# Routed experts in order of kept tokens, with a 224-wide and a 96-wide second item

## The chip, the cores and the metric

The kernel runs on one core of a Trainium2 chip. The metric is device time of one execution in microseconds (us). Three timed executions of the kernel before gave 530.63, 530.70 and 531.04 us, median 530.7 us. A profile is one more execution, with its own time.

## The reference

Three layers in a row, in float32: attention with rotary positions over 2 batches of 576 tokens (8 heads of 64), a dense feed-forward layer 512 to 2048 to 512, and a layer of 8 routed experts, each 512 to 1024 to 512. The last is what this case is about:

```
    logits = x @ w_gate                      # 1152 tokens, 8 experts
    expert_idx = np.argmax(logits, axis=1)
    ...
    for i in range(N):
        e = expert_idx[i]
        if counts[e] < capacity:             # capacity = 288
            disp[e, counts[e]] = x[i]
            ...
    h = np.maximum(np.einsum('ecd,edf->ecf', disp, w1), 0.0)
    y = np.einsum('ecf,efd->ecd', h, w2)
    out[i] = gate_w[i] * y[expert_idx[i], pos[i]]   # kept tokens; the rest stay 0
```

The reference with its inputs sends the first 576 tokens to two experts (212 tokens to expert 3, 364 to expert 5, of which 288 are kept) and the second 576 to two others (509 to expert 0, of which 288 are kept, 67 to expert 4). So 855 rows of the output are written, and 297 stay zero.

## The kernel before

*Stages.* Attention; then the dense layer in three chunks of 480, 384 and 288 tokens (blocks of 96 tokens, CUTS), 16 slices of its hidden width each; then up to four routed *items* in straight code, and a loop (line 1048) for items that did not fit into them. An item is one expert with up to 288 slots (HALF). Of the 576 tokens of a batch the routing fills two items: items 0 and 1 after block 6 (in chunk 3's time), items 2 and 3 after chunk 3. With these inputs the items hold 212, 288, 288 and 67 tokens, in the order of the experts' numbers, and the loop runs zero times. Each item computes all 288 columns, whatever it holds.

*One item* (`second`, with `ffn`). Eight slices. A slice is one weight load of 512 KB (`wf`, line 965, issued by SP), cut into a high and a low float32r half (`hl`: line 671 on ACT, 672 on DVE), 12 matmuls into `h` (line 696; the high and low products over 4 blocks of 128), `gh` on ACT (721) and `gl` on DVE (722), and 12 matmuls into the four accumulators `y` (line 706). After the last slice `yt` copies (983), 12 transposes `tr` (991), three scalings by the gate (`row`, 997 and 999) and three indirect scatters to `out` (1000) on POOL. A slice's load is issued no earlier than the cut of the slice six before it (LEAD).

*Routing* (`route`, lines 776 to 920). A chain of some 74 short DVE operations, with matmuls for the ranks in between, from the logits to `r_at`, the slot of each token; then six indirect writes to the table `slots` in DRAM from POOL (871). On one partition DVE also makes `etab` (the expert of each item, 892) and `n`, the number of items (920).

*Gather.* SP loads an item's part of the table (`ent`, line 927: 288 slots of 16 bytes), POOL gathers three blocks of 96 rows (`got`, line 932), PE transposes them (`tg`, 949, four for each block) and ACT and DVE split them into `xt` (955, 956). Those transposes stand two slices before the end of the item ahead (`hook`).

*Order.* A scheduler writes each engine's order at build time, by a model of durations; instructions of one engine start in that order. SP's order holds the weight loads, the block stores `x<-row` (761), the `ent` loads and the loads of expert numbers (1013), POOL's the indirect DMAs. So a waiting `ent` load on SP holds the weight loads behind it.

Of the kernel before, what the change touches and what calls it, by code (L numbers as in the profile page):

```python
# [24 lines left out]
P = 128  # L25
# [8 lines left out]
ITEMS = 4 + 14  # L34
# [70 lines left out]
def consts():  # L105
# [16 lines left out]
    for b in range(B):  # L122
# [11 lines left out]
        (e[None, :] < e[:, None]).reshape(-1),  # L134
        np.repeat(np.arange(16)[:, None], E, 1).reshape(-1),
        np.repeat(e[None, :], 16, 0).reshape(-1),
        np.arange(16),
# [455 lines left out]
class Experts:  # L593


    def __init__(self, ctx, tc, d, cst, xt, weights):
# [19 lines left out]
        self.small = one.tile([TT, 48 + 64 + 128 + 128 + 16], F32, name="small")  # L616
# [5 lines left out]
        self.etab = one.tile([1, 20], I32, name="etab")  # L622
        self.loc = one.tile([1, B, 16], F32, name="loc")
        self.small_parts = {}
        at = 0
        for n, shape in (("rev", (NT, E)), ("low", (E, E)), ("k", (16, E)), ("e", (16, E)), ("i", (16,))):
# [47 lines left out]

    def ffn(self, x, slices, act, hook=None):
# [6 lines left out]
        for f in range(n + LAG):  # L682
# [4 lines left out]
            if f < n:  # L687
                hl = hls[f]
                h = self.ps_h.tile([P, 512], F32, tag="h", name="h")[:, 0:w]
                ops = [  # L690
                    (hl[:, i, j * P:(j + 1) * P], x[:, k, j, :])
                    for j in range(ND)
                    for i, k in ((0, 0), (0, 1), (1, 0))
                ]
                for m, (u, v) in enumerate(ops):
                    nc.tensor.matmul(h, u, v, start=m == 0, stop=m == len(ops) - 1)  # L696
                gh = self.g.tile([P, WIDE], F32R, name="gh")[:, 0:w]
                gl = self.g.tile([P, WIDE], F32R, name="gl")[:, 0:w]
                act(h, gh, gl, f)
                gs.append((gh, gl))  # L700
# [25 lines left out]
    def first(self, k0, k1, hook=None):  # L726
# [17 lines left out]
        for k in range(k0, k1):  # L744
            b, i = divmod(k, NT)
            cs = slice((k - k0) * TT, (k - k0 + 1) * TT)
            row = self.three.tile([TT, DM], F32, name="row")
# [15 lines left out]
    def route(self, b, L):  # L763
# [20 lines left out]

        big, col = lambda n: new(n, NT, E), lambda n: new(n, NT)
        big16 = lambda n: new(n, NT, E, dt=BF16)
        mx = col("mx")
        red(mx, L, ALU.max)
        ls, ex, sm, gate = big("ls"), big("ex"), col("sm"), col("gate")
        tt(ls, L, per(mx), ALU.subtract)  # L790
        nc.scalar.activation(out=ex, in_=ls, func=AF.Exp)
        red(sm, ex)
        ts(sm, sm, 1e-9, ALU.add)
        v.reciprocal(out=gate, in_=sm)
        sc, fm, oh = big("sc"), col("fm"), big("oh")
# [12 lines left out]
        found = oh16.rearrange("p (a k) e -> p a k e", a=2)  # L808
# [12 lines left out]
        cnt, left, tmp, tmp2 = new("cnt", E), new("left", E), big("tmp"), big("tmp2")  # L821
        v.tensor_copy(out=cnt, in_=pc[0:TT, 0:E])
        ts(left, self.carry, -1.0, ALU.mult, self.cap, ALU.add)
        tt(self.carry, self.carry, cnt, ALU.add)
        tt(tmp, rank, oh, ALU.mult)
        lr, keep = col("lr"), col("keep")
        red(lr, tmp)
        tt(tmp2, rank, every(left), ALU.is_lt)
        tt(tmp2, tmp2, oh, ALU.mult)
        red(keep, tmp2)  # L830
        kc, items, base = new("kc", E), new("items", E), new("base", E)
        ts(kc, left, 0.0, ALU.max)
        tt(kc, kc, cnt, ALU.min)
        ts(items, kc, 0.0, ALU.is_gt)
        more = new("more", E)
        ts(more, kc, float(HALF), ALU.is_gt)
        tt(items, items, more, ALU.add)
        sq = new("sq", E, E)
        tt(sq, sp["low"], items.unsqueeze(1).to_broadcast([TT, E, E]), ALU.mult)
        red(base, sq)  # L840
        ends, ni = new("ends", E), new("ni", 1)
        tt(ends, base, items, ALU.add)
        red(ni, items)
        jb, over = col("jb"), col("over")
        tt(tmp, oh, every(base), ALU.mult)
        red(jb, tmp)
        ts(over, lr, float(HALF), ALU.is_ge)
        tt(jb, jb, over, ALU.add)
        slot, few = col("slot"), col("few")
        ts(few, jb, 2.0, ALU.is_lt)  # L850
        off = new("off", 1)
        ts(off, self.xoff, -1.0, ALU.mult, 2.0 * b - 2.0, ALU.add)
        ts(few, few, off, ALU.mult)
        ts(few, few, self.xoff, ALU.add, 2.0, ALU.add)
        tt(slot, jb, few, ALU.add)
        tt(slot, slot, over, ALU.subtract)
        v.scalar_tensor_tensor(out=slot, in0=over, scalar=1.0, in1=slot, op0=ALU.mult, op1=ALU.add)
        ts(slot, slot, float(HALF), ALU.mult)
        tt(slot, slot, lr, ALU.add)
        ts(over, over, float(HALF), ALU.mult)  # L860
        tt(slot, slot, over, ALU.subtract)
        ts(keep, keep, -float(FAR), ALU.mult, float(FAR), ALU.add)
        tt(slot, slot, keep, ALU.add)
        at = new("at", NT, dt=I32)
        placed = v.tensor_copy(out=at, in_=slot)
# [16 lines left out]
        with self.tc.issue_after(placed.ins):  # L882

            k, e = sp["k"][0:1], sp["e"][0:1]
            m1, m2 = new("m1", 16, E, part=1), new("m2", 16, E, part=1)
            lo, hi = (x[0:1].unsqueeze(1).to_broadcast([1, 16, E]) for x in (base, ends))
            tt(m1, k, lo, ALU.is_ge)
            tt(m2, k, hi, ALU.is_lt)
            tt(m1, m1, m2, ALU.mult)
            tt(m1, m1, e, ALU.mult)  # L890
            red(self.loc[:, b], m1)
            v.tensor_copy(out=self.etab[:, 2 * b:2 * b + 2], in_=self.loc[:, b, 0:2])
            if b == 0:
                ts(self.xoff, ni, -2.0, ALU.add, 0.0, ALU.max)
                return

            x0 = self.xoff[0:1]
            z1 = new("z1", 16, part=1)
            lo2, hi2 = new("lo2", E, part=1), new("hi2", E, part=1)
            tt(lo2, base[0:1], x0.to_broadcast([1, E]), ALU.add)  # L900
            tt(hi2, ends[0:1], x0.to_broadcast([1, E]), ALU.add)
            lo, hi = (x.unsqueeze(1).to_broadcast([1, 16, E]) for x in (lo2, hi2))
            tt(m1, k, lo, ALU.is_ge)
            tt(m2, k, hi, ALU.is_lt)
            tt(m1, m1, m2, ALU.mult)
            tt(m1, m1, e, ALU.mult)
            red(z1, m1)
            late, lim = new("late", 16, part=1), new("lim", 1, part=1)
            ts(lim, x0, 2.0, ALU.add)
            ts(late, sp["i"][0:1], lim, ALU.is_ge)  # L910
# [3 lines left out]
            tt(z1, z1, late, ALU.add)  # L914
            v.tensor_copy(out=self.etab[:, 4:18], in_=z1[:, 2:16])
            n1 = new("n1", 1, part=1)
            ts(n1, ni[0:1], -2.0, ALU.add, 0.0, ALU.max)
            tt(n1, n1, x0, ALU.add)
            ts(n1, n1, 4.0, ALU.add)
            v.tensor_copy(out=self.etab[:, 18:19], in_=n1)  # L920
# [103 lines left out]
    def run(self):  # L1024
# [4 lines left out]
        def turn(i):  # L1029
            x[i] = self.turn(found[i][1], i)  # L1030
# [51 lines left out]
```

## Time and profile before

| | |
|---|---|
| timed, median of 3 | 530.7 us (530.63 to 531.04) |
| the profiled execution's own time | 531.68 us |
| its span in the trace | 530.0 us |
| PE busy | 489.3 us, 92% |
| DVE, ACT, POOL busy | 374.1, 275.7, 112.9 us |
| HBM, mean over the span | 97 GB/s |
| mean granted clock of TensorE | 0.983 of 2.4 GHz |

The span ends when the last instruction of the trace does; 1.68 us of the execution's own time lie around it. PE is the busiest engine in every stage but the last, so a place where PE stands still, or runs at half its clock, shows as time, and so does each matmul that goes. The matmuls overlap: the duration of one says less than the distance from start to start of a run of the same shape. In a row of the timeline `[2.28 <-DMA got<-x,ent]` means that the engine was idle 2.28 us before it, and what ended that.

### The profile page before, as it was taken

To read this page: it belongs to the slowest core of one execution; us is meant where nothing else is said; L and a number is where in the kernel's file an instruction comes from. 1 tells how busy PE (TensorE), PEld (TensorE's weight loads), DVE (VectorE), ACT (ScalarE), POOL (GpSimd) and SP (SyncE) were. 2 spreads that over 40 slices of the span, in tenths; PEclk is the share of its full clock that TensorE was granted. 3 is DMA by queue.
4 is the path that set the end of the run, shared out by engine and by line. 5 is a ranking of instruction groups with operands and counts; after the bars stand their busy time and mean duration, and the time that the engine had idled before them with its cause. 6 is when DMAs were issued, how large, how long until landed. Compare 5 with 4: busy or idle time off the path is not lost.

```text
span 530.0 us, 8969 instructions
## 1 busy us (share of the span) xinstructions
PE 489.3 (92%) x3306; PEld 440.8 (83%) x3306; DVE 374.1 (71%) x761; ACT 275.7 (52%) x520; POOL 112.9 (21%) x119
## 2 busy tenths in 40 slices
PE   1889999999999999999999999999899996999991
PEld 0768778778777788788899999999899985999991
DVE  6798898898789999998355343677456873565631
ACT  3567678667557534345543444655464532645421
POOL 5964534322211200000000000002510073120202
PEclk9999999999999999999999999999989997999996
DMA  7042332222043475661011400010495427564200
GB/s 246 0 110 77 101 94 67 79 51 71 4 130 121 151 278 179 238 238 41 0 31 53 171 1 1 16 46 2 142 288 151 153 58 228 177 190 153 86 1 14
DMA packets 21535, 56.16 MB, mean 106 GB/s; under 512 B 4996, under 2 KB 6180, under 8 KB 21488
## 3 DMA queue, kind: packets, MB, share of 16 engines
q1 hardware_dynamic: 19136, 50.91, 30.4%
q0 software_dynamic: 1920, 4.13, 2.8%
q8 instruction: 28, 0.46, 0.4%
q10 hardware_dynamic: 432, 0.51, 0.3%
q14 instruction: 19, 0.16, 0.1%
HBM read 44.38 MB, written 7.18 MB: 97 GB/s over the span
## 4 chain that ended last, share of the span: by engine, by line
PE 41%; issue 25%; DVE 17%; DMA 8%; ACT 4%; POOL 4%; POOLq 0%; SPq 0%; ACTq 0%; DVEq 0%
PE h L696 13%; PE y L706 12%; PE s L392 6%; PE pv L492 4%; DVE nm L396 3%; PE tp L441 3%; DMA raw<-in_w_in 2%; DMA qx<-qs 2%; DVE hl L297 2%; POOL out L1000 2%; PE tr L752 2%; DMA got<-x,ent 1%; POOL slots L871 1%; ACT pp L403 1%; DMA raw<-in_w_out 1%
## 5 line engine op out<-in xcount | busy, mean ns | idle before, releaser
L696 PE MATMUL h<-xt,hl 128*128 128x288 f32 (+2 forms) x960 | 181.1, 326 | 2.4 <-issue 1.8
L696 PEld LDWEIGHTS h<-xt,hl 128*128 128x128 f32 x960 | 152.2, 190 | 10.8 <-issue 3.3
L706 PE MATMUL y<-gh,hl 128*128 128x288 f32 (+2 forms) x640 | 142.0, 325 | 2.4 <-issue 2.0
L672 DVE TENSOR_TENSOR hl<-wf,hl 128x1024 fp32r<-128x1024 f32 x80 | 97.7, 1224 | 62.4 <-ACT hl L671 61.0
L671 ACT ACTIVATE hl<-wf 128x1024 fp32r<-128x1024 f32 x80 | 84.5, 1059 | 60.6 <-PE y L706 34.6
L706 PEld LDWEIGHTS y<-gh,hl 128*128 128x128 f32 x640 | 108.4, 191 | 5.9 <-issue 1.7
L706 PE MATMUL y<-gl,hl 128*128 128x288 f32 (+2 forms) x320 | 89.7, 324 | 1.1 <-issue 1.1
L396 DVE TENSOR_REDUCE nm<-s 128x1 f32<-128x576 f32 x72 | 53.8, 752 | 12.0 <-PE s L392 10.7
L706 PEld LDWEIGHTS y<-gl,hl 128*128 128x128 f32 x320 | 58.7, 191 | 3.5 <-issue 1.7
L403 ACT ACTIVATE pp<-s,nm 128x576 f32<-128x576 f32 x64 | 47.7, 745 | 23.9 <-DVE nm L396 23.4
L871 POOL DMA_INDIRECT slots<-entry,r_at x12 | 13.5, 1124 | 218.6 <-DVE r_m L776 180.8
L715 ACT ACTIVATE g<-h 128x480 f32<-128x480 f32 (+2 forms) x48 | 23.4, 490 | 61.0 <-PE h L696 50.2
L392 PE MATMUL s<-ks,qs 128*128 128x288 f32 (+1 forms) x168 | 53.0, 333 | 2.0 <-ACT pp L403 1.6
L392 PE MATMUL s<-ks,qx 128*128 128x288 f32 (+1 forms) x168 | 46.9, 306 | 3.2 <-DMA qx<-qs 2.4
L211 ACT ACTIVATE pt<-tp 128x512 f32<-128x512 f32 x56 | 33.1, 599 | 19.6 <-PE tp L441 19.0
L717 DVE TENSOR_TENSOR gl<-g,gh 128x480 fp32r<-128x480 f32 (+2 forms) x48 | 26.5, 554 | 22.2 <-ACT gh L716 22.0
L441 PE MATMUL tp<-ident,pp 128*128 128x128 f32 x256 | 39.8, 281 | 0.5 <-DVE ptr L213 0.5
L492 PE MATMUL pv<-pt,vr 128*64 128x288 f32 x256 | 39.1, 414 | 0.6 <-DVE pt L213 0.3
L392 PEld LDWEIGHTS s<-ks,qs 128*128 128x128 f32 x168 | 32.6, 195 | 8.2 <-ACT pp L403 3.6
L721 ACT ACTIVATE gh<-h 128x288 fp32r<-128x288 f32 x32 | 13.2, 412 | 45.8 <-PE h L696 31.9
L392 PEld LDWEIGHTS s<-ks,qx 128*128 128x128 f32 x168 | 32.8, 196 | 4.6 <-DMA qx<-qs 2.0
L441 PEld LDWEIGHTS tp<-ident,pp 128*128 128x128 f32 x256 | 30.5, 143 | 5.3 <-issue 2.6
(178 smaller groups left out, 593.3 us busy)
## 6 DMA issues: line engine op xcount, KB each, us to landing
wf<-in_w SPq DMA_DIRECT2D x32, 512.0 KB, 4.1
raw<-in_w_in SPq DMA_DIRECT2D x16, 512.0 KB, 3.9
raw<-in_w_out SPq DMA_DIRECT2D x16, 512.0 KB, 3.3
qx<-qs SPq DMA_DIRECT2D x14, 320.0 KB, 4.2
qk<-in_qk SPq DMA_DIRECT2D x12, 288.0 KB, 3.1
vr<-in_v SPq DMA_DIRECT2D x8, 320.0 KB
x<-row SPq DMA_DIRECT2D x12, 192.0 KB, 2.1
out<-zero SPq DMA_DIRECT2D x9, 256.0 KB, 2.9
```

Of the source, the lines that this page charges most:

```text
L211: return e.activation(out=out, in_=x, func=AF.Copy, **({} if scale is None else {"scale": scale}))
L392: nc.tensor.matmul(ps[:, n, c:c + w], x, ks[:, src:src + w], start=j == 0, stop=j == len(mine) - 1)
L396: nc.vector.tensor_reduce(out=nm, in_=ps[:, :, 0:HALF], axis=AX.XY, op=ALU.max, negate=True)
L403: nc.scalar.activation(out=out.rearrange("p (n k) -> p n k", n=2), in_=ps[:, :, 0:HALF], func=AF.Exp, bias=d["nm"][:, i:i + 1], accum_out= ...
L441: nc.tensor.transpose(t[:, kt], pp[:, h, h * 64 + kt * P:h * 64 + (kt + 1) * P], self.ident)
L492: nc.tensor.matmul(o[h * 64:h * 64 + 64], x, y, start=j < 2, stop=j > 7)
L671: nc.scalar.activation(out=hl[:, 0], in_=t, func=AF.Copy)
L672: self.last = nc.vector.tensor_tensor(out=hl[:, 1], in0=t, in1=hl[:, 0].bitcast(F32), op=ALU.subtract).ins
L696: nc.tensor.matmul(h, u, v, start=m == 0, stop=m == len(ops) - 1)
L706: nc.tensor.matmul(y[j][:, 0:w], u, v, start=f == LAG and m == 0, stop=f == n + LAG - 1 and m == 2)
L715: nc.scalar.activation(out=g, in_=h, func=AF.Gelu_apprx_sigmoid)
L717: nc.vector.tensor_tensor(out=gl, in0=g, in1=gh.bitcast(F32), op=ALU.subtract)
```

## The change

Seven parts.

1. Items of a batch are ordered by kept tokens (most first; `key`, `sq`), not by the number of the expert.
2. STATIC gives each of the four items its blocks: items 0 and 2 three of 96 tokens, item 1 two of 112 (224 columns), item 3 one of 96. Tokens of a second item beyond 224 or 96 go to an item of the loop (`more`, `extra`, `s1`, `s2`).
3. Item 3 is computed token-major (`few`): `y` is 96 tokens x 512, with `gh` and `gl` as the stationary operand and 512 columns of the weights moving, 3 matmuls a slice instead of 12; no `yt`, no `tr`; the scaling is halved between ACT and DVE; one scatter.
4. The routing chain is shorter: 57 operations up to `r_at` instead of 74. The gate's exponent, sum and reciprocal come after `r_at`.
5. `ent` loads are issued by POOL, not SP.
6. The number of an item's expert is loaded by SP without waiting for `ent` to have been issued.
7. The transposes `tg` may stand up to the end of the item ahead (hook 0 instead of 2).

```diff
+STATIC = (3, 96), (2, 112), (3, 96), (1, 96)
...
-        tt(sq, sp["low"], items.unsqueeze(1).to_broadcast([TT, E, E]), ALU.mult)
+        stt(key, kc, float(E), ALU.mult, sp["e"][:, 0, :], ALU.subtract)
+        wide = [TT, E, E]
+        tt(sq, key.unsqueeze(1).to_broadcast(wide), key.unsqueeze(2).to_broadcast(wide), ALU.is_gt)
+        tt(sq, sq, items.unsqueeze(1).to_broadcast(wide), ALU.mult)
         red(base, sq)
...
+        ts(back, ni, -float(HALF), ALU.mult, float(HALF + narrow), ALU.add)
+        ts(over, self.xoff, float(HALF), ALU.mult, float((2 - 2 * b) * HALF), ALU.add)
+        tt(over, over, back, ALU.subtract)
+        ts(s1, lin, float(first + HALF + narrow), ALU.is_ge, over, ALU.mult)
+        ts(s2, lin, float(first + 2 * HALF), ALU.is_ge, back, ALU.mult)
+        tt(lin, lin, s1, ALU.add)
+        tt(lin, lin, s2, ALU.add)
...
-        ent = self.three.tile([TT, 3, 4], I32, name="ent", bufs=5)
-        src = self.slots[bass.ds(item * HALF, HALF), :].rearrange("(i p) c -> p i c", p=TT)
-        self.told = (nc.sync if len(batches) == 1 else nc.gpsimd).dma_start(out=ent, in_=src)
+        ent = self.three.tile([P, 3, 4], I32, name="ent", bufs=5)[0:size, 0:blocks]
+        src = self.slots[bass.ds(item * HALF, blocks * size), :].rearrange("(i p) c -> p i c", p=size)
+        nc.gpsimd.dma_start(out=ent, in_=src)
...
+    def few(self, ent, x, expert):
+        size = ent.shape[0]
+        y = self.ps_y.tile([P, 512], F32, tag="y0", name="y0")[0:size]
...
+            if f >= LAG:
+                hl, (gh, gl) = hls[f - LAG], gs[f - LAG]
+                for m, (u, i) in enumerate(((gh, 0), (gh, 1), (gl, 0))):
+                    nc.tensor.matmul(
+                        y, u, hl[:, i, DM:], start=f == LAG and m == 0, stop=f == n + LAG - 1 and m == 2
+                    )
+        row = self.three.tile([P, DM], F32, name="row")[0:size]
+        gate = ent[:, 0, 3:4].bitcast(F32)
+        nc.scalar.activation(out=row[:, 0:256], in_=y[:, 0:256], func=AF.Copy, scale=gate)
+        nc.vector.tensor_scalar(out=row[:, 256:], in0=y[:, 256:], scalar1=gate, scalar2=None, op0=ALU.mult)
+        self.send(ent, 0, row)
...
-            self.first(k0, k1, {0: (10, self.setup), len(CUTS) - 2: (2, lambda: turn(0))}.get(n))
+            self.first(k0, k1, {0: (10, self.setup), len(CUTS) - 2: (0, lambda: turn(0))}.get(n))
...
-        for i in range(4):
-            with tc.issue_after(told[i].ins):
-                expert = self.expert(i, sp)
-            self.second(found[i][0], x[i], expert, (2, lambda: turn(i + 1)) if i < 3 else None)
+        for i in range(3):
+            self.second(found[i][0], x[i], self.expert(i, sp), (0, lambda: turn(i + 1)))
+        self.few(found[3][0], x[3], self.expert(3, sp))
```

How the order moves, at the three places on which the steps below rest. First PE at the end of the dense layer's third chunk; `tg` are the transposes of item 0's gathered rows, `h` and `y` the chunk's matmuls. Before:

```order
L696 MATMUL h<-xt,hl 128x288 x8
L949 MATMUL tg<-ident,got 128x96 x4
L696 MATMUL h<-xt,hl 128x288 x2
L706 MATMUL y_3778<-gl,hl 128x288
L706 MATMUL y_3779<-gh,hl 128x288
```

Now, one hidden slice later:

```order
L963 MATMUL tg<-ident,got 128x96
L686 MATMUL h<-xt,hl 128x288 x10
L963 MATMUL tg<-ident,got 128x96 x7
L712 MATMUL y_3769<-gh,hl 128x288 x2
L712 MATMUL y_3769<-gl,hl 128x288
```

The first block's transposes stood inside the hidden matmuls of slice 14, with two hidden slices' work half open; now one stands ahead of the last ten hidden matmuls of slice 15 and seven behind them.

Second, POOL from the routing of the second batch on: `slots` the writes to the table, `ent` the loads from it, `got` the gathers, `out` the scatters. Before (the `ent` loads are on SP):

```order
L871 DMA slots<-entry,r_at 5184x4 x6
L1000 DMA out<-row,ent 1152x512 x3
L932 DMA got<-x_2193,ent 96x512 x6
L1000 DMA out<-row,ent 1152x512 x9
L1047 TENSOR_LOAD etab
```

Now:

```order
L868 DMA slots<-entry,r_at 5760x4 x6
L940 DMA ent<-slots 96x3x4
L940 DMA ent<-slots 96x4
L987 DMA out<-row,ent 1152x512
L945 DMA got<-x_2193,ent 96x512 x3
L987 DMA out<-row,ent 1152x512
L945 DMA got<-x_2193,ent 96x512
L987 DMA out<-row,ent 1152x512 x7
```

Two of item 0's three scatters went behind gathers, and the `ent` loads stand right behind the writes that they read.

Third, PE in item 1, around the first transposes of item 2's rows; `h` and `y` are item 1's. Before:

```order
L696 MATMUL h<-xt,hl 128x288 x10
L949 MATMUL tg<-ident,got 128x96 x4
L706 MATMUL y_4921<-gh,hl 128x288 x2
L706 MATMUL y_4922<-gh,hl 128x288 x2
L696 MATMUL h<-xt,hl 128x288 x3
L949 MATMUL tg<-ident,got 128x96 x4
```

Now:

```order
L712 MATMUL y_4896<-gl,hl 128x224
L963 MATMUL tg<-ident,got 128x96
L686 MATMUL h<-xt,hl 128x224 x10
L712 MATMUL y_4893<-gh,hl 128x224 x2
L712 MATMUL y_4893<-gl,hl 128x224
L712 MATMUL y_4894<-gh,hl 128x224 x2
```

The first of them stood behind 120 of item 1's 192 matmuls; now it stands behind 86, and those have 224 columns.

## Rows read from the trace of the kernel before

**Rows 1.** Windows: us, busy us (xcount) by engine, granted clock, DMA share, GB/s.
```profile
366.00:395.00 29.00, 26.72 (x193) 26.27 (x191) 15.28 (x25) 16.35 (x29) 13.19 (x12) 0.94 0.57 174
...
437.00:446.00 9.00, 3.97 (x17) 2.73 (x16) 1.34 (x2) 1.32 (x3) 5.01 (x5) 0.84 0.84 244
446.00:463.00 17.00, 17.00 (x120) 17.00 (x120) 10.43 (x14) 9.85 (x17) 2.22 (x2) 0.88 0.59 177
...
490.00:517.00 27.00, 27.00 (x207) 26.93 (x205) 12.68 (x18) 9.73 (x18) 2.74 (x3) 1.00 0.14 43
```

**Rows 2.** Timeline of PE, end of chunk 3: start, duration, work, idle before.
```profile
383.60 0.55 PE L949 MATMUL tg<-ident,got 96*128 96x96 f32 x4 [2.28 <-DMA got<-x,ent]
...
387.38 0.44 PE L706 MATMUL y<-gl,hl 128*128 128x288 f32 x1
387.62 0.68 PE L706 MATMUL y<-gh,hl 128*128 128x288 f32 x2
```

**Rows 3.** Timeline of PE, items 0 to 3, for the distances between starts.
```profile
423.05 0.49 PE L949 MATMUL tg<-ident,got 96*128 96x96 f32 x4
423.33 0.64 PE L706 MATMUL y<-gh,hl 128*128 128x288 f32 x3
...
424.47 0.43 PE L696 MATMUL h<-xt,hl 128*128 128x288 f32 x2
...
429.72 0.60 PE L991 MATMUL tr<-ident,yt 128*96 128x128 f32 x4
430.07 1.30 PE L706 MATMUL y<-gh,hl 128*128 128x288 f32 x8
...
433.34 1.23 PE L706 MATMUL y<-gh,hl 128*128 128x288 f32 x8
434.41 1.76 PE L696 MATMUL h<-xt,hl 128*128 128x288 f32 x12
...
490.33 2.43 PE L696 MATMUL h<-xt,hl 128*128 128x288 f32 x17
```

**Rows 4.** Timeline of PE, attention, matmuls of 224 and of 64 columns.
```profile
45.72 0.28 PE L392 MATMUL s<-ks,qx 128*128 128x224 f32 x1
45.83 0.20 PE L392 MATMUL s<-ks,qs 128*128 128x64 f32 x1
45.87 0.28 PE L392 MATMUL s<-ks,qx 128*128 128x64 f32 x1
```

**Rows 5.** Groups of lines on DVE, 426 to 463 us: busy us, mean ns.
```profile
L672 DVE TENSOR_TENSOR hl<-wf,hl 128x1024 fp32r<-128x1024 f32 x8 | 9.7, 1222 | 6.9 <-ACT hl L671 5.7 <-issue 1.2
L722 DVE SCALAR_TENSOR_TENSOR gl<-h,gh 128x288 fp32r<-128x288 f32 x8 | 3.6, 450 | 10.3 <-ACT gh L721 7.5 <-issue 2.8
...
L776 DVE TENSOR_TENSOR r_z<-r_z,r_late 1x16 f32<-1x16 f32 x2 | 0.3, 158 | 0.0
```

**Rows 6.** Timeline of POOL: both routings, and the last scatter.
```profile
373.47 0.92 POOL L871 DMA_INDIRECT slots<-entry,r_at  x1 [0.30 <-issue]
378.11 0.98 POOL L932 DMA_INDIRECT got<-x,ent  x1 [3.72 <-DMA ent<-slots]
...
425.39 0.97 POOL L871 DMA_INDIRECT slots<-entry,r_at  x1 [34.81 <-DVE r_at L865]
426.67 2.60 POOL L871 DMA_INDIRECT slots<-entry,r_at  x1 [0.30 <-issue]
...
521.64 0.92 POOL L1000 DMA_INDIRECT out<-row,ent  x1 [0.30 <-issue]
```

**Rows 7.** Timeline of SP, both routings.
```profile
375.49 0.84 SPq L927 DMA_DIRECT2D ent<-slots  x2
...
435.81 0.86 SPq L927 DMA_DIRECT2D ent<-slots  x2
439.55 4.33 SPq L965 DMA_DIRECT2D wf<-in_w  x3
```

**Rows 8.** Timeline of PE between 438 and 446 us.
```profile
441.00 0.29 PE L706 MATMUL y<-gl,hl 128*128 128x288 f32 x1 [1.11 <-issue]
```

More of the change, by code (lines that the diff above doesn't have):

```diff
@@ L688, in ffn @@
                 hl = hls[f]
[L689 to L700, printed above, removed]
+                gs.append(self.hidden(hl, x, act, f))
             if f >= LAG:
@@ L840, in route @@
         red(base, sq)
-        ends, ni = new("ends", E), new("ni", 1)
-        tt(ends, base, items, ALU.add)
+        ts(at0, base, float(HALF), ALU.mult, float(first), ALU.add)
         red(ni, items)
[L844 to L851, printed above, removed]
@@ L882, in route @@
         with self.tc.issue_after(placed.ins):
[L884 to L892, printed above, removed]
+            k, e, idx = sp["k"][0:1], sp["e"][0:1], sp["i"][0:1]
@@ new lines, in route, with owners @@
+            m1, m2 = new("m1", ROWS, E, part=1), new("m2", ROWS, E, part=1)
+            ends = each("ends")
+            tt(ends, base, items, ALU.add)
+            def owners(out, lo, hi):
+                lo, hi = (x[0:1].unsqueeze(1).to_broadcast([1, ROWS, E]) for x in (lo, hi))
+                tt(m1, k, lo, ALU.is_ge)
+                tt(m2, k, hi, ALU.is_lt)
+                tt(m1, m1, m2, ALU.mult)
+                tt(m1, m1, e, ALU.mult)
+                red(out, m1)
+            loc = self.loc[:, b]
@@ L893, in route @@
+            owners(loc, base, ends)
+            v.tensor_copy(out=self.etab[:, 2 * b:2 * b + 2], in_=loc[:, 0:2])
+            full, more, extra = each("full"), new("more", 1), new("extra", ROWS, part=1)
+            stt(full, base, float(HALF), ALU.mult, kc, ALU.add)
+            ts(full, full, float(HALF + narrow), ALU.is_gt)
+            stt(full, base, 2.0, ALU.is_lt, full, ALU.mult)
+            red(more, full)
+            x0 = self.xoff[0:1]
             if b == 0:
+                ts(extra, idx, ni[0:1], ALU.is_equal, more[0:1], ALU.mult)
+                stt(loc, extra, loc[:, 1:2], ALU.mult, loc, ALU.add)
+                tt(ni, ni, more, ALU.add)
@@ L903, in route @@
[L903 to L908, printed above, removed]
+            owners(z1, lo2, hi2)
+            last = new("last", 1, part=1)
+            tt(last, ni[0:1], x0, ALU.add)
+            ts(extra, idx, last, ALU.is_equal, more[0:1], ALU.mult)
+            stt(z1, extra, loc[:, 1:2], ALU.mult, z1, ALU.add)
@@ L944, in turn @@
         nc = self.nc
[L945 removed]
+        size = rows[0].shape[0]
+        x = self.xt[:, :, :, k * HALF:k * HALF + len(rows) * size]
         for i, row in enumerate(rows):
@@ L959, in second, with send @@
+    def send(self, ent, i, row):
+        ins = self.nc.gpsimd.indirect_dma_start(
+            out=self.d["out"],
+            out_offset=bass.IndirectOffsetOnAxis(ap=ent[:, i, 2:3], axis=0),
+            in_=row,
+            in_offset=None,
+            bounds_check=N - 1,
+            oob_is_err=False,
+        )
+        for x in self.sent:
+            self.tc.declare_no_dep(ins.ins, x.ins, reason="each token has a row of its own")
+        self.sent.append(ins)
     def second(self, ent, x, expert, hook=None):
@@ L984, in second @@
-        for i in range(3):
-            cs = slice(i * TT, (i + 1) * TT)
-            if last and i == 2:
-                t = self.ps_h.tile([P, 512], F32, tag="h", name="h")
-            else:
-                t = self.ps_m.tile([P, 512], F32, tag="m", name="tr")
+            nc.scalar.activation(out=yt[:, j, 0:w], in_=y[j][:, 0:w], func=AF.Copy)
+        for i in range(blocks):
+            cs = slice(i * size, (i + 1) * size)
+            t = self.ps_m.tile([P, 512], F32, tag="m", name="tr")
@@ L1000, in second @@
-            ins = nc.gpsimd.indirect_dma_start(
-                out=self.d["out"],
-                out_offset=bass.IndirectOffsetOnAxis(ap=ent[:, i, 2:3], axis=0),
-                in_=row,
-                in_offset=None,
-                bounds_check=N - 1,
-                oob_is_err=False,
-            )
-            for x in self.sent:
-                self.tc.declare_no_dep(ins.ins, x.ins, reason="each token has a row of its own")
-            self.sent.append(ins)
+            nc.vector.tensor_scalar(out=row, in0=t[0:size, :], scalar1=gate, scalar2=None, op0=ALU.mult)
```

192 lines of the change are left out of this document (95 added, 97 removed).

## The prediction

> **What bounds the kernel now.** I read the windows first, then PE's timeline at the places where a window shows PE short of its time, then the queues that PE waited for. In the windows [rows 1] PE is busy all the time in items 2 and 3 (27.00 of 27.00 us from 490 to 517), so there a matmul that goes is time saved. It is short in two places. At the end of chunk 3 it waits 2.28 us for gathered rows [rows 2], and behind that wait runs at half its clock: starts lie 0.24 us apart (387.38 to 387.62) where eight matmuls of the same shape take 1.07 us at full clock (433.34 to 434.41 [rows 3], 0.134 each). And from 437 to 446 us PE does 17 matmuls in 9 us, at 244 GB/s and a DMA share of 0.84 [rows 1]; its timeline steps at over 1 us with nothing named but "issue" [rows 8]. The last stage is the tail of item 3: the last scatter is issued at 521.64 [rows 6], 31.3 us after item 3's first matmul at 490.33 [rows 3]; what follows it is the scatter's landing, 8.4 us to the span's end, which I leave as it is.
>
> **End of chunk 3: -3.9 us.** The chain to `r_at` loses 17 of 74 operations; short ones take about 0.16 us each [rows 5], so some 2.7 us. `ent` goes from SP to POOL: before, the last table write was issued at 373.47, `ent` at 375.49, the first gather at 378.11 [rows 6, 7]. If POOL is as quick as SP was, the first rows come near 380.7 instead of 383.6, and PE asks for them one hidden slice later, at about 383. The wait (2.28) goes, and with it the half clock behind it: from 385.1 to 388.6 some 15 matmuls at 0.24 instead of 0.134, 1.6 us. Bounds: 0 if `ent` on POOL takes 3 us longer than on SP, -3.9 if all goes.
>
> **Item 1 at 224 columns: -5.4 us, and small transposes -1.1.** The 224-column matmul of attention starts 0.11 us before its successor (45.72 to 45.83 [rows 4]; over two of them 0.105), a 288-column one 0.134. 8 slices x 24 matmuls x 0.028 = 5.4 us. DVE covers it only just: in item 1 it has 8 cuts of 1.222, 8 `gl` of about 0.37 (0.450 at 288 columns) [rows 5], and with three scalings, the `xt` halves and the tail of the second routing that makes about 21 us against PE's 22. I add 1 us of waits (0 to 3). Transposes: four `tg` take 0.28 us (423.05 to 423.33), four `tr` 0.35 (429.72 to 430.07) [rows 3]. Item 1 has 8 `tg` of 112 for 12 of 96 (-0.2) and one `tr` group less (-0.35), item 3 eight `tg` less (-0.56).
>
> **Item 3 token-major: -16.9 us.** PE: 96 hidden matmuls of 96 columns, 24 `y` of 512. No row has a stream of 96-column matmuls in this form. Nearest: 64 columns, 0.04 us to the next start (45.83 to 45.87 [rows 4]); and a `tg`, which also moves 96 columns past 128 of weights, 0.07 [rows 3]. `tr`, 128 columns, takes 0.088. I take 0.07, with 0.04 and 0.088 as ends: 6.7 us (3.8 to 8.4). 512 columns by scale from 288: 0.134 x 512 / 288 = 0.24, 24 of them 5.7 us. Item 2's 12 `tr`, which lie in this stretch as before, 1.05. Together 13.5; plus 0.3 for a wait on cuts, since DVE needs 8 x (1.222 + 0.25) = 11.8 and item 2's three scalings 2.2, of which three or four cuts (up to 4.9) lie ahead of the item; plus 0.6 from the last matmul to the scatter's issue (half a `row`, then POOL). That is 14.4 us against 31.3. Ends: 11.5 and 16.5. The weights are no limit: a load goes six cuts ahead, and the stretch of item 3 had a DMA share of 0.14 [rows 1].
>
> The Trainium skill, "TensorE: Matmul & The Clock Gate", section "LDWEIGHTS (loading the stationary operand)", speaks against so narrow a moving side: it prices a weight load at its columns over 1.2, which is an estimate of 107 ns for 128 columns, however few columns move. By that page the 96 hidden matmuls would take 10.2 us and the item about 18. The rows at 0.04 and 0.07 us, each with its own load of 128 columns, do not agree, and I go by them.
>
> **A new wait in item 1: +3, and +1 for the clock.** The first `tg` of item 2 now stands behind 86 matmuls of item 1 instead of 120, and those are shorter. Item 1 began at 424.47 [rows 3]; 86 x 0.105 and its four `tr` groups put PE there at about 434.9, in the clock of before. The rows: `r_at` some 3.5 us earlier (2.7, and a cut of DVE less in between), so the first table write at about 421.9 instead of 425.39 [rows 6], six at about 1.25, issued by 429; landed at 430 (373.47 + 0.92 to 375.49 was 1.1); two `ent` loads and one `out` on POOL at 1.2 each (the pitch of its indirect DMAs), gather at 433.4 to 434; rows 2.6 us later if a gather lands like an `ent` load (375.49 to 378.11), 5.5 if like the first gather of chunk 3 (378.11 to 383.60). So 436 to 439.5; PE waits 1 to 4.6, I take 3. Queued behind the `tg` on PE are the rest of item 1's matmuls, so all of it is time. Ends: 0 if DVE already holds PE back, 8 if a table write again takes 2.60 [rows 6] and an `ent` of 288 slots costs three such writes. The clock behind a wait of that size cost 1.6 at chunk 3; I take 1 (0 to 2).
>
> The Trainium skill, "SBUF — State Buffer", section "Who interferes with whom", has a rule against part of this edit: a DMA issued by GpSimd can be held up while DVE holds the port that they share, and one from SP can't. By it the two `ent` loads, in a stretch where DVE is nearly full, come later than I say; the one write at 2.60 us among those of 0.92 and 0.97 [rows 6] may be that. It is the third rival.
>
> **The stall from 437 to 446: -8.5 us if it goes.** 17 matmuls are 2.3 us of 9, so 6.7 are lost; and 446 to 463 has a mean clock of 0.88 [rows 1], 4.1 of 17 us at half, another 2.0 of which I count 1.8. In it met: two `ent` loads from SP (435.81), the three scatters of item 0, the gathers from 438.61, and the weight loads of item 2, which SP had held behind `ent` and let go together from 439.55 [rows 7]. Now SP holds nothing behind `ent`, the table loads have 384 slots instead of 576, and scatters and gathers alternate. For "gone" speaks that no other stretch of the items has it, and that the DMA share there is the highest. Against it: in chunk 3 the same `ent`, gathers and a row of weight loads met at a share of 0.57 with no such steps, so what makes it is not shown. I take it as gone, with a chance only a little over one half.
>
> **The sum,** on the profiled execution's 531.68 us: -3.9 -5.4 -1.1 -16.9 +1 +3 +1 = 509.4; -8.5 = 500.9. That execution lies 1.0 above the timed median (530.7), so 499.9, which I call 500. What moves and costs nothing: the gate's operations after `r_at` (on DVE behind the table writes, off PE's path as long as `row` of items 0 and 2 stays later), the load of `n` on SP (behind two loads of item 2, which have over 10 us to come).
>
> **Rivals.**
> 1. The stall stays, or another collision of the same size takes its place. For it: its cause isn't shown, and the gathers and weight loads still meet. It then swallows part of the new wait: 500 + 8.5 - 1 to 3 = 506 to 508.
> 2. No new wait: gathered rows are there when PE asks. Then 500 - 4 = 496; if the narrow matmuls also go at 0.04, 493.
> 3. `ent` on POOL comes late (port or queue): the wait in item 1 is 8 and the one at chunk 3 stays: 500 + 5 + 3.9 = 508 to 510.
> 4. Slower: the loop runs. A second item of over 224 kept tokens, or over 96 in the second batch, sends its rest to a loop item of 288 columns that has nothing loaded ahead: `ent` and gather 2.6 + 5.5, 27 us of matmuls, 8 to 10 of first loads and cuts, the transposes: some 45 us, so 545. It decides from token 225 or 97 on. The reference's counts are 212 and 67, so only a mistake in the counts, or other inputs, would bring it; and a fault in the new chain that counts one item too many would too.
>
> **How the numbers follow.** Forecast 0.5 (its own range 497 to 504), rival 1 0.24, rival 2 0.1, rival 3 0.13, rival 4 0.03. Predicted 500. The range 493 to 510 takes the first four but for their far ends. A measurement of this kernel can tell about 0.2%, 1.1 us: every case but the fourth is far faster. Faster 0.96, same 0.01, slower 0.03.
>
> **What would show it.** After: item 3 from its first hidden matmul to the scatter's issue about 14 us; item 1's matmuls at 0.105; no wait at the first `tg` of chunk 3 and a clock of 1.0 there; an idle time of some 3 us ahead of the first `tg` in item 1, released by a gather; no window below 90% PE between 430 and 450. Wrong if PE again steps at over 1 us with "issue", if narrow matmuls take 0.1 us each, or if PE's gaps in item 3 drop its clock to half, which would double its 12 us of matmuls.

## The result, and the profile after

The changed kernel took 509.69 us (median of four runs, 507.78 to 513.69) where the kernel before took 530.66: a ratio of 0.9623, 95% interval 0.9557 to 0.9689. A second set of six runs gave 510.44. Every ratio below is against the kernel before on the same chip, where its median lay between 530.7 and 533.6. Forecast were 500, the forecast's own range 497 to 504, the range with the rivals 493 to 510. The direction was right and a third of the gain did not come: the time lies above the forecast's own range, at the price of rival 3 (508 to 510). The profiled execution took 510.73 us, its span is 508.9.

By stages, from the timelines of both (from a stage's first hidden matmul to the next one's, the last to the issue of the last scatter; in the kernel before one hidden matmul of item 2 stands alone at 460.81, and the stage is counted from the others, at 462.54):

| stage | before | after | difference | forecast |
|---|---|---|---|---|
| up to chunk 3 (unchanged code) | 329.4 | 332.2 | +2.9 | 0 |
| chunk 3 | 64.8 | 64.4 | -0.4 | -3.9 |
| item 0 | 30.3 | 30.0 | -0.4 | -0.2 |
| item 1 | 38.1 | 28.1 | -10.0 | -8.9 |
| items 2 and 3 | 59.1 | 45.4 | -13.7 | -17.8 |
| landing of the last scatter | 8.4 | 8.9 | +0.6 | 0 |

The first row is spread between executions: a second profile of the same kernel had it at 329.2 and a span of 505.9. What has to be explained is chunk 3 (3.5 us), items 2 and 3 (4.1 us), and what lies under item 1's figure, since that it comes near the forecast is luck: parts that were foreseen otherwise happen to add up to it.

The windows of the changed kernel, columns as in [rows 1]:

```profile
366.00:395.00 29.00, 25.79 (x197) 25.56 (x196) 15.76 (x31) 15.20 (x27) 13.43 (x13) 1.00 0.48 160
426.00:437.00 11.00, 8.57 (x62) 8.38 (x61) 6.88 (x20) 4.37 (x9) 5.78 (x6) 0.84 0.56 152
437.00:446.00 9.00, 9.00 (x84) 9.00 (x83) 6.44 (x14) 5.36 (x8) 7.35 (x6) 1.00 0.69 205
```

The stretch that was nearly empty before is full, 84 matmuls instead of 17; but PE is short by 3.2 us in the first window and by 2.4 in the second, at a mean clock of 0.84 there. The first loss, on PE, DVE, POOL and SP (timelines; idle time before in brackets):

```profile
379.80 0.54 PE L712 MATMUL y<-gl,hl 128*128 128x288 f32 x2 [3.21 <-DVE gl L723]
```
```profile
379.21 0.18 DVE L864 COPY entry<-rows 96x24 int32<-96x24 int32 x1 [6.92 <-DMA slots<-entry,r_at]
379.30 0.45 DVE L723 TENSOR_TENSOR gl<-g,gh 128x288 fp32r<-128x288 f32 x1
```
```profile
373.38 0.92 POOL L868 DMA_INDIRECT slots<-entry,r_at  x1 [0.30 <-issue]
379.37 1.42 POOL L940 DMA_DIRECT2D ent<-slots  x2 [5.07 <-DMA slots<-entry,r_at]
```
```profile
370.28 30.01 SPq L975 DMA_DIRECT2D wf<-in_w  x10
```

They are read from the last to the first. SP, no longer behind `ent`, starts item 0's weight loads at 370.28, while POOL is still writing the table. The last write is issued by 374.30 and has landed only by 379.2, 5 us later, where it took 1.1 before [rows 6, 7], with no weight load under way. Two things wait for it: the table load on POOL, and a copy on DVE that prepares the entries of the *second* batch in the same tile. `gl` stands behind that copy on DVE, and PE behind `gl`. The gathered rows, which PE waited for before [rows 2], are in time.

The second loss, at the start of item 1, PE and ACT:

```profile
426.56 0.38 PE L686 MATMUL h<-xt,hl 128*128 128x224 f32 x2
429.36 0.51 PE L1012 MATMUL tr<-ident,yt 128*96 128x128 f32 x2 [2.43 <-issue]
...
430.56 3.06 PE L686 MATMUL h<-xt,hl 128*128 128x224 f32 x15
433.46 0.38 PE L1012 MATMUL tr<-ident,yt 128*96 128x128 f32 x2
...
441.69 0.25 PE L963 MATMUL tg<-ident,got 96*128 96x96 f32 x1
```
```profile
428.89 1.45 ACT L1007 ACTIVATE yt<-y 128x288 f32<-128x288 f32 x4 [1.84 <-remote]
```

PE waits for `tr`, `tr` for `yt`, and ACT stands 1.84 us ahead of `yt` for something that the profile doesn't name. Behind the stop 15 matmuls of 224 columns take 2.90 us, 0.19 each, where they take 0.112 later. At the first `tg` of item 2, 441.69, there is no wait: PE came there 15.1 us after item 1's first matmul (426.56), where the forecast had 10.4 (424.47 to 434.9).

Item 3, the columns as before:

```profile
493.59 1.44 PE L686 MATMUL h<-xt,hl 128*128 128x96 f32 x12
494.87 0.43 PE L1033 MATMUL y<-hl,gl 128*96 128x512 f32 x1
495.14 0.62 PE L1033 MATMUL y<-hl,gh 128*96 128x512 f32 x2
495.59 1.44 PE L686 MATMUL h<-xt,hl 128*128 128x96 f32 x12
```

Twelve hidden matmuls of 96 columns take 1.28 us from start to start, 0.107 each, not 0.07. Three of 512 columns take 0.72 (494.87 to 495.59), 0.24 each as forecast. PE is busy all through, at a granted clock of 1.00. From its last matmul to the scatter it is 1.3 us (498.70 to 499.99), where the sum had 0.6:

```profile
498.30 0.40 PE L1033 MATMUL y<-hl,gl 128*96 128x512 f32 x1
```
```profile
499.99 0.92 POOL L987 DMA_INDIRECT out<-row,ent  x1 [9.50 <-DVE row L1039]
```

### The profile page after: what moved, and what is told of

Read it like the earlier page. It is cut to its first block, busy times and chain, and to the rows that moved or that the text cites. A ratio compares the mean times of both kernels' runs of the same rounds, so it can differ in the third digit from the quotient of the medians.

```text
span 508.9 us, 8730 instructions
## 1 busy us (share of the span) xinstructions
PE 469.6 (92%) x3206; PEld 420.2 (83%) x3206; DVE 366.8 (72%) x746; ACT 272.1 (53%) x515; POOL 112.8 (22%) x117
## 3 DMA queue, kind: packets, MB, share of 16 engines
q1 hardware_dynamic: 17920, 50.91, 31.3%
## 4 chain that ended last, share of the span: by engine, by line
PE 53%; DVE 13%; issue 13%; DMA 10%; ACT 5%; POOL 3%; SPq 0%; POOLq 0%; DVEq 0%; ACTq 0%
PE h L686 19%; PE y L712 17%; PE s L393 6%; PE pv L493 4%; DMA qx<-qs 3%; PE tp L442 2%; DMA raw<-in_w_in 2%; DVE nm L397 2%; PE tr L758 2%; DMA raw<-in_w_out 2%; DVE hl L298 2%; POOL out L987 1%; ACT pp L404 1%; DMA slots<-entry,r_at 1%; POOL slots L868 1%
## 5 line engine op out<-in xcount | busy, mean ns | idle before, releaser
L686 PE MATMUL h<-xt,hl 128*128 128x288 f32 (+4 forms) x960 | 175.2, 321 | 2.0 <-DVE hl L673 1.9
L686 PEld LDWEIGHTS h<-xt,hl 128*128 128x128 f32 x960 | 148.7, 191 | 10.9 <-DVE hl L673 3.1
L712 PE MATMUL y<-gh,hl 128*128 128x288 f32 (+3 forms) x576 | 123.9, 322 | 0.4 <-ACT gh L722 0.4
L712 PEld LDWEIGHTS y<-gh,hl 128*128 128x128 f32 x576 | 94.9, 188 | 4.3 <-ACT gh L722 0.8
L712 PE MATMUL y<-gl,hl 128*128 128x288 f32 (+3 forms) x288 | 77.2, 322 | 3.2 <-DVE gl L723 3.2
L868 POOL DMA_INDIRECT slots<-entry,r_at x12 | 14.7, 1221 | 209.2 <-ACT hl L672 178.0
L712 PEld LDWEIGHTS y<-gl,hl 128*128 128x128 f32 x288 | 50.7, 188 | 5.5 <-DVE gl L723 3.7
L727 ACT ACTIVATE gh<-h 128x288 fp32r<-128x288 f32 (+2 forms) x32 | 11.5, 358 | 38.0 <-PE h L686 38.0
```

Source lines behind the costliest of these rows:

```text
L686: self.nc.tensor.matmul(h, u, v, start=m == 0, stop=m == len(ops) - 1)
L712: nc.tensor.matmul(y[j][:, 0:w], u, v, start=f == LAG and m == 0, stop=f == n + LAG - 1 and m == 2)
```

## The experiments

Theory A was that the two stops on PE, at the copy of the entries and in item 1, and the price of a narrow matmul make up what is missing. The theories against it stand in the expectations.

**Two entry tiles.**

```diff
-        entry = self.one.tile([TT, NT, 4], I32, name="entry")
+        entry = self.one.tile([TT, NT, 4], I32, name=f"entry{b}")
```

> The changed kernel with a tile of its own for each batch's table entries. In the changed kernel's trace DVE stands 6.92 us at the copy of the second batch's entries, which waits for the first batch's six table writes, and PE 3.21 us behind it (375.9 to 379.8). Theory A (the wait of that copy is what stopped PE at the end of chunk 3): the copy no longer waits, no idle time of PE over 1 us between 365 and 395, and 2.5 to 3.5 us less than the changed kernel, so about 505 to 507. Rival B (the weight loads of item 0, which now start before the table writes have landed, hold up whatever is in chunk 3): the table writes land as late, the gathered rows too, and PE waits elsewhere for as long; the time stays at 508 to 511.

509.76 us (507.03 to 510.89), ratio 0.9584 (0.9555 to 0.9613): no faster than the changed kernel that can be told. But its trace, which is that of its fastest run (507.03), lost the first stop, and has another one. Windows, PE, POOL:

```profile
366.00:395.00 29.00, 28.98 (x222) 28.57 (x221) 17.67 (x31) 17.98 (x31) 11.31 (x12) 1.00 0.58 202
```
```profile
436.28 0.39 PE L963 MATMUL tg<-ident,got 96*128 96x96 f32 x1 [4.76 <-DMA got<-x,ent]
436.38 2.46 PE L686 MATMUL h<-xt,hl 128*128 128x224 f32 x10
438.63 0.63 PE L712 MATMUL y<-gh,hl 128*128 128x224 f32 x2
```
```profile
423.26 1.24 POOL L868 DMA_INDIRECT slots<-entry,r_at  x1 [0.31 <-issue]
428.77 1.28 POOL L940 DMA_DIRECT2D ent<-slots  x2 [4.27 <-DMA slots<-entry,r_at]
430.35 0.97 POOL L987 DMA_INDIRECT out<-row,ent  x1 [0.30 <-DVE gl L728]
432.08 1.11 POOL L945 DMA_INDIRECT got<-x,ent  x1 [0.76 <-PE y L712]
```

Chunk 3 is 60.9 us instead of 64.4, as A says. The stop ahead of `yt` is gone too. What comes in its place is the wait that the forecast had put there: 4.76 us for gathered rows, and half the clock behind it (10 matmuls in 2.25 us). Of the chain, the gather itself took 4.2 us (432.08 to 436.28), the landing of the table writes over 4 again (from 424.50 to 428.77). From the first table write to the first `tg` it is 20.1 us here and 19.3 in the changed kernel: PE comes to that `tg` about as long after the routing in both, by a wait in the one and by the stops ahead of it in the other.

**Weights behind the table load.** The first load of item 0 (`hold`) waits until item 0's `ent` has landed.

```diff
+            self.hold = told[0] if i == 0 else None
...
+        if getattr(self, "hold", None) is not None:
+            self.tc.add_manual_dep(
+                ins.ins, self.hold.ins.name, mybir.DependencyInfo(mybir.DependencyClass.Sync, mybir.DependencyReason.DATA), reason="held"
+            )
+            self.hold = None
```

> The changed kernel, but the first weight load of item 0 (and so all loads behind it on SP) waits until item 0's table load has landed. Theory A says that the table writes waited behind weight loads at 380 to 430 GB/s: here they land within 1.5 us of the last issue as before, POOL's table load follows at once (in the changed kernel it waited 5.07 us), DVE waits under 1.5 us at the copy of the entries instead of 6.92, and PE loses under 1 us there, so 505 to 508. Rival B (table writes on POOL's queue are slow in themselves, or the copy waits for something else): the table load still waits 4 to 5 us and the time is 508 to 511 or more, since the weights come later.

514.7 us (512.5 to 517.7), ratio 0.9678 (0.9644 to 0.9712): no faster than the changed kernel (0.9623), where theory A had put it 2 to 5 us faster. POOL and PE:

```profile
374.27 1.42 POOL L940 DMA_DIRECT2D ent<-slots  x2 [1.38 <-DMA slots<-entry,r_at]
```
```profile
384.16 0.35 PE L963 MATMUL tg<-ident,got 96*128 96x96 f32 x2 [2.85 <-DMA got<-x,ent]
...
445.07 0.39 PE L963 MATMUL tg<-ident,got 96*128 96x96 f32 x1 [7.69 <-DMA got<-x,ent]
```

The mechanism is confirmed: without weight loads in flight the table load waits 1.38 us instead of 5.07. The time isn't: the copy of the entries still held DVE 3.2 us, though PE lost nothing there, and the weights, starting at 376.40, now met the gather, whose rows came 7 us after its issue at 377.20. Here, who goes first only moved the collision. The second routing, where nothing was edited, had a wait of 7.69 this time.

**The kernel before with its weight loads freed.**

```diff
-            with tc.issue_after(told[i].ins):
-                expert = self.expert(i, sp)
+            expert = self.expert(i, sp)
```

> The kernel before with one edit of the change alone: the loads of an item's expert number, and so its weight loads, no longer stand behind the item's table loads on SP. Theory A: at the first routing the same collision as in the changed kernel (table writes over 4 us from the last issue to the load that needs them, DVE held at the copy of the entries for 3 to 7 us); at the second routing the weight loads of item 2 come spread out instead of at once from 439.55, and the steps of over 1 us from 437 to 446 go or shrink to under 4 us: time 523 to 530. Rival C (that stall came from the table loads, the scatters and the gathers on the queues, not from the weight loads let go at once): the steps stay, 8 us lost, and the time is 529 to 535.

532.87 us, ratio 1.0015 (0.9994 to 1.0035): the same. POOL and SP at the first routing, and PE:

```profile
373.47 1.57 POOL L871 DMA_INDIRECT slots<-entry,r_at  x1 [0.30 <-issue]
```
```profile
379.61 0.86 SPq L927 DMA_DIRECT2D ent<-slots  x2
```

```profile
390.81 0.69 PE L949 MATMUL tg<-ident,got 96*128 96x96 f32 x4 [2.81 <-DMA got<-x,ent]
...
448.22 0.52 PE L949 MATMUL tg<-ident,got 96*128 96x96 f32 x4 [3.81 <-DMA got<-x,ent]
451.89 0.88 PE L949 MATMUL tg<-ident,got 96*128 96x96 f32 x4 [3.14 <-DMA got<-x,ent]
```

A was right on the table writes. In this kernel SP's order has six and seven weight loads ahead of the `ent` loads; the last of them was issued well before, and then SP waited for the writes. The first `ent` load came 4.57 us after the last write's issue had ended (375.04 to 379.61) instead of 1.1, at the second routing 4.37 (435.52 to 439.89). So the late landing shows in the kernel before too, by this one edit. A's part on DVE failed: the copy of the entries did not wait, it stood later in DVE's order.

The steps of over 1 us are gone, as A said; two waits for gathered rows, 7.0 us together, have come in their place. What made the steps stays open: they go with this edit, but it has two effects, and the trace before speaks against the loads let go at once:

```profile
437.82 0.53 PE L696 MATMUL h<-xt,hl 128*128 128x288 f32 x2 [0.46 <-issue]
...
439.59 0.30 PE L706 MATMUL y<-gh,hl 128*128 128x288 f32 x1 [0.97 <-issue]
```

Both of these stops of PE began before the first of those loads was issued, at 439.55. And SP stepped too: three loads took it 4.33 us [rows 7], where four take 3.66 with the loads freed (from 442.15).

**Item 3 at 72 slots.**

```diff
-STATIC = (3, 96), (2, 112), (3, 96), (1, 96)
+STATIC = (3, 96), (2, 112), (3, 96), (1, 72)
```

> The changed kernel with 72 instead of 96 slots in item 3 (67 tokens are kept). If a narrow matmul costs what its weight load of 128 columns costs (in the changed kernel 12 of 96 columns take 1.28 to 1.36 us, 0.107 to 0.113 each), the 12 hidden matmuls of a slice take the same 1.28 us and item 3 changes by under 0.5 us: 508 to 511. If a narrow matmul is paid by its moving columns, they take 0.96 us, item 3 is 2.5 us shorter: 505 to 508, with 12 matmuls in under 1.05 us in the trace.

513.39 us; items other than 3 took the difference (item 1 34.3 us, with a wait of over 7 us for gathered rows). Item 3 itself took 18.6 us, with 96 slots 18.7:

```profile
499.65 1.43 PE L686 MATMUL h<-xt,hl 128*128 128x72 f32 x12
500.90 0.43 PE L1033 MATMUL y<-hl,gl 128*72 128x512 f32 x1
```

12 matmuls in 1.25 us, 0.104 each: a quarter of the columns less saved nearly nothing. From 72 to 96 to 224 moving columns such a matmul goes from 0.104 to 0.107 to 0.112 us, so in this stretch it is not paid by what moves. That the load of its weights is the price fits, but a fixed price of each matmul would look the same: every matmul here has a load of its own.

**Late transposes**, with two entry tiles. `tg` of item 2 behind the last hidden matmul of item 1:

```diff
+            if i == 2:
+                with tc.issue_after(self.h_last.ins):
+                    x[i] = self.turn(found[i][1], i)
```

> The kernel with two entry tiles, and item 2's transposes ordered behind the last hidden matmul of item 1 (some 3 us of matmuls ahead of item 2). In the trace of the two entry tiles PE waits 4.76 us for gathered rows at the first of these transposes and runs the next 10 matmuls at half clock (1.1 us). Theory A (that wait is what is left of the loss in item 1): both go, no idle time of PE over 1 us from 426 to 446, 4 to 6 us less than with two entry tiles alone: 503 to 506. Rival B (the gather chain is late in any case, and the stop moves to the start of item 2): PE waits 2 us or more at the end of item 1, 507 to 510.

504.33 us (502.73 to 505.10), ratio 0.9470 (0.9437 to 0.9503): A, 5.4 us less than with two entry tiles alone by the medians. (The two traces are only 2.5 us apart, since the one of the two entry tiles is that of its fastest run.) Windows:

```profile
366.00:395.00 29.00, 28.98 (x223) 28.57 (x222) 17.68 (x31) 17.97 (x31) 12.85 (x12) 1.00 0.59 201
426.00:437.00 11.00, 11.00 (x101) 11.00 (x100) 8.29 (x18) 5.67 (x8) 5.18 (x6) 1.00 0.66 227
437.00:446.00 9.00, 8.23 (x74) 7.73 (x72) 6.03 (x9) 6.78 (x13) 3.35 (x4) 1.00 0.93 295
446.00:463.00 17.00, 16.23 (x111) 16.01 (x112) 7.91 (x12) 5.83 (x10) 2.62 (x2) 0.90 0.43 133
```

PE is full until 437. Two smaller waits (0.84 and 0.69) and some half clock are left at the start of item 2. The runs also lie closer, 2.4 us apart instead of 6; that the changed kernel's spread came from the gather chain is not shown.

**Late transposes with one entry tile**, and the changed kernel again:

> The changed kernel with item 2's transposes behind the last hidden matmul of item 1, and one entry tile as in the changed kernel. If the two stops are two losses, only that of item 1 goes: about 3 us slower than the late transposes with two entry tiles (504.3), so 506 to 509, with DVE over 4 us at the copy of the entries in the trace. If the wait at the copy costs nothing because item 1 waits for the gather chain anyway, it is within 1.5 us of 504.3.

> The changed kernel as it is, on the chip of the next one, since its runs lay 6 us apart (507.8 to 513.7). If the two stops in its trace (3.21 us in chunk 3, 2.43 us and a half clock in item 1) come every time, the median is 509 to 512 and its trace again shows DVE over 4 us at the copy of the entries and, in item 1, either a wait for gathered rows of 4 us or more or a stop of like size ahead of it. If the trace before was an odd one, the median is under 508 and one of the two is missing.

510.72 us (508.46 to 512.19), ratio 0.9572, for the first, 510.44 (507.56 to 514.79), ratio 0.9593, for the second. Alone, then, neither edit gains (509.76 and 510.72); together they gain 6. With one entry tile the trace has the stop at the copy (3.06 us on PE) and the one ahead of `yt`, PE comes to the transposes late, and moving them later saves nothing. The expectation of 506 to 509 took the two losses for independent, and missed. The second profile of the changed kernel had both stops again (3.27 and 2.27 us), so the first was no odd one. The stop ahead of `yt` is in three traces of the four changed kernels whose copy waits with weights in flight (the one with 72 slots waited 7.4 us at `tg` instead) and in none of the four with two tiles and item 1 at 224 columns; what ACT waited for, and how the one makes the other, is not shown.

**Merged products in item 3**, on the late transposes with two tiles:

```diff
+        for j in range(ND):
+            nc.tensor.matmul(both, hl[:, 0, j * P:(j + 1) * P], x[:, :, j, :], start=j == 0, stop=False)
+            nc.tensor.matmul(h[:, 0:w], hl[:, 1, j * P:(j + 1) * P], x[:, 0, j, :], start=False, stop=j == ND - 1)
...
+        nc.scalar.activation(out=low, in_=h[:, w:2 * w], func=AF.Copy)
+        nc.vector.tensor_tensor(out=s, in0=h[:, 0:w], in1=low, op=ALU.add)
```

> As the late transposes, and in item 3 the products of the high half of the weights with the high and the low half of the tokens are one matmul of 192 columns, so 8 hidden matmuls a slice instead of 12 (the two halves of the accumulator are added on ACT and DVE, two operations of 96 columns more a slice). If a narrow matmul costs its weight load, 4 of 12 loads go: 0.42 us a slice, 3.4 us in all, 0.5 us of which the longer chain takes back: 500 to 503. If columns are what is paid (as many columns as before), or DVE and ACT bound the item: no gain, 503 to 506.

503.06 us (501.62 to 505.54), against 504.33: 1.3 less, and the ranges of the runs overlap.

```profile
481.74 0.40 PE L1050 MATMUL y<-hl,gl 128*96 128x512 f32 x1
...
482.96 0.31 PE L699 MATMUL h<-xt,hl 128*128 128x96 f32 x1 [0.28 <-DVE hl L673]
483.11 0.32 PE L698 MATMUL h<-xt,hl 128*128 128x192 f32 x1
483.27 0.23 PE L699 MATMUL h<-xt,hl 128*128 128x96 f32 x1
483.33 0.32 PE L698 MATMUL h<-xt,hl 128*128 128x192 f32 x1
...
484.80 0.33 PE L698 MATMUL h<-xt,hl 128*128 128x192 f32 x1 [0.59 <-DVE g L703]
```

A pair takes 0.22 us (483.11 to 483.33), so 8 matmuls take 0.88 and the saving on PE is there. But PE now waits for DVE instead (0.28, 0.59), which has one more operation a slice, and item 3 gained nothing: from its first matmul to the scatter it is 20.8 us here and 20.4 with the late transposes alone. The difference of the two traces lies elsewhere: at the start of item 2, which is the same in both, 22 matmuls of 288 columns took 3.01 us here and 4.55, in good part at half the clock, there. So the expectation's second case came, no gain. It is the lowest median of all, 0.9464 (0.9428 to 0.9500) of the kernel before, but not one that can be told from the late transposes (0.9470).

**Item 3 computed as the other items**, with two entry tiles:

```diff
-        self.few(found[3][0], x[3], self.expert(3, sp))
+        self.second(found[3][0], x[3], self.expert(3, sp))
```

> The kernel with two entry tiles, item 3 at 96 columns but computed as the other items are: 12 matmuls of 96 columns into y for each slice instead of 3 of 512, then yt, 4 transposes, one scaling. At 0.107 us a narrow matmul, y costs 96 x 0.107 = 10.3 us instead of 24 x 0.23 = 5.5, and the tail 1 to 1.5 us more: 5 to 6.5 us slower than with two entry tiles, 514 to 517. At 0.07 us a matmul it would be 6.7 against 5.5, and 511 to 513.

525.3 us (522.79 to 526.45): 15.5 slower, against 5 to 6.5 expected. Item 3 took 34.8 us, longer than before with 288 columns. Windows and PE:

```profile
480.00:490.00 10.00, 10.00 (x94) 10.00 (x92) 6.35 (x10) 4.68 (x11) 3.49 (x3) 1.00 0.30 94
490.00:491.00 1.00, 1.00 (x11) 1.00 (x10) 0.43 (x1) 0.54 (x1) 0.00 (x0) 1.00 0.59 168
491.00:513.00 22.00, 22.00 (x108) 22.00 (x107) 4.18 (x7) 3.88 (x9) 0.00 (x0) 0.51 0.01 2
```
```profile
489.27 0.39 PE L712 MATMUL y<-gh,hl 128*128 128x96 f32 x2
...
498.78 2.76 PE L686 MATMUL h<-xt,hl 128*128 128x96 f32 x12
501.34 0.84 PE L712 MATMUL y<-gl,hl 128*128 128x96 f32 x3
```

PE has no idle time, and from 491 its clock is at half all the same: 12 matmuls take 2.56 us, 0.213 each. So the token-major form was worth much more here than its fewer matmuls: in the changed kernel, with matmuls of 512 columns between the narrow ones, item 3 kept the full clock (1.00 from 480 to 499).

**Item 1 at 288 columns**, on the late transposes with two tiles:

```diff
-STATIC = (3, 96), (2, 112), (3, 96), (1, 96)
+STATIC = (3, 96), (3, 96), (3, 96), (1, 96)
```

> As the late transposes, with item 1 at three blocks of 96 (288 columns) instead of two of 112. With 0.134 us for a matmul of 288 columns and 0.1115 for one of 224 (the changed kernel's trace), 192 x 0.0225 = 4.3 us more, and 0.5 for transposes: 4 to 5.5 us slower than the late transposes alone. If the wait for gathered rows still bounds item 1, the wider matmuls fill that wait and the difference is under 2 us.

512.14 us, 7.8 slower than the late transposes. Not to be read as the price of the width alone: its start of item 1 has two new waits for `xt` (1.01 and 1.26 us) and half a clock behind them, where item 1's own transposes, three blocks now, are split into `xt`. From the traces, 0.134 against 0.112 us a matmul, the width is 4.3 us.

## Why the prediction was right and wrong

Of the 9.8 us between the sum (500.9) and the profiled execution (510.73), 4.1 lie in items 2 and 3 and 3.5 in chunk 3, where two steps of the prediction failed; 2.9 are spread ahead of chunk 3, 0.6 the last landing, and items 0 and 1 give 1.3 back.

- *Item 3, -16.9: mis-sized.* From 31.3 us it came to 18.7, not to 14.4. The step took a narrow matmul at 0.07 us, from `tg`, with 0.04 from one successor in attention as the lower end; measured were 0.107 at 96 columns and 0.104 at 72. For 96 matmuls that is 3.6 us, and the tail added 0.7. The prediction had named this sign itself (wrong "if narrow matmuls take 0.1 us each"). The two rows misled: `tg` is another form, and the distance from a short matmul behind a longer one to its successor is no price. In the merged products the 192-column matmul is followed after 0.16 us, the 96-column one behind it after 0.06, and the mean is 0.11. The Trainium skill, "TensorE: Matmul & The Clock Gate", section "LDWEIGHTS (loading the stationary operand)", gave an estimate of 107 ns for a load of 128 columns, from which the prediction had worked out an item of about 18 us; the trace has 0.107 and 18.7. The forecast weighed the page against rows of another situation and chose wrongly. The 512-column matmuls came as worked out; the wait on cuts (0.3) did not come.
- *Chunk 3, -3.9: failed.* The step followed the chain to the gather and found it earlier; it did not ask what the weight loads that SP no longer held back would meet. They met the table writes, 5 us from issue to landing instead of 1.1, and a copy on DVE that the sum had not in it. The wait of 2.28 went, as forecast, and 3.21 came. The entry-tile run shows that without it chunk 3 is 60.9 us: 3.9 less than before, the forecast to the tenth, but by another edit and partly by luck, since there too the table load waited 4.7 us for the writes. The step's own bound gave nothing for an `ent` 3 us late; the rows were in time all the same, because PE asked for them later (at 384.65 in that trace).
- *The new wait in item 1, +3 and +1 for the clock: right in kind, too small.* It was 4.8 and 5.8 us with two entry tiles, 7.4 and 7.7 in the two one-tile kernels without a stop ahead of `yt`. The step had put the table writes' landing at 1.1; it took 4.3 to 4.5 in these four. In the changed kernel the stop ahead of `yt` covers the wait.
- *The stall at 437, -8.5: right that it goes.* The window is full. What the step lacked is that the gather chain lay under it: freeing the weights in the kernel before removed the steps and gained nothing. Its reading that SP let the loads of item 2 go together is not what the row says, three in 4.33 us [rows 7].
- *Item 1 at 224, -5.4: nearly.* 0.112 us instead of 0.105, so 4.3.
- *Rivals.* Rival 3 has the number (508 to 510) and half of the mechanism: `ent` did come late, by the landing of the writes ahead of it. What chunk 3 lost by it came over DVE's copy, though, not over late rows. Rival 1's other collision came too, in another place. Rival 2 did not, but for the stop that covers the wait; nor did rival 4 (545): the trace has nine scatters, those of the four items.
- *The port.* The rule of the Trainium skill, "SBUF — State Buffer", section "Who interferes with whom", that the prediction put behind rival 3 was not seen at work on `ent`: two `ent` loads took 1.3 to 1.4 us of POOL, and what made them late was the landing of the writes ahead of them. What made single table writes long (2.04 and 1.80 us of POOL at the first routing) is not shown.
- *Slips in the sum,* none of which moves the forecast by more than 0.4 us: item 0 has three groups of `tr`, not four; 383.6 less 2.7 is 380.9, not 380.7; the upper end of item 3 adds up to 16.1, not 16.5.

## What to carry to other kernels

When a wait is taken from a queue, list what the queue then starts earlier and which small transfers are in flight at that moment: here 512 KB loads that nobody needed for 20 us made writes of 16 bytes a row take 5 us to land, and a tile shared by two uses turned that into a stop of PE. Price a narrow matmul from a run of its own form, not by its columns: in these runs narrowing below 224 columns gained next to nothing. Merging two that share weights saved PE 0.4 us a slice, and the time only as far as no other engine takes over, which here it did. Two waits in a row on one chain are not a sum: remove both before judging either.

## What the runs showed of the hardware

- A float32r matmul that brings 128 columns of weights cost 0.104 us at 72 moving columns, 0.107 at 96, 0.112 at 224, 0.134 at 288; one that brings 96 columns of weights 0.24 at 512.
- The granted clock fell to half (1.2 GHz) with PE busy without a gap, in a run of 96-column matmuls alone (0.51 over 22 us); with matmuls of 512 columns among them it was 1.00.
- Indirect writes of 16 bytes a row landed 1.1 to 1.7 us after the end of their issue with no weight load under way (the kernel before at both routings, and the weights held back), and 3.2 to 5.2 us after it beside weight loads from SP, in the changed kernels and in the kernel before with its weight loads freed.
